# Loading K and V two units at a time: 1 MB transfers, four ring and five kept buffers, and another mix of phases

## The chip, the cores and the metric

The kernel runs on one core of one Trainium2 chip. The metric is the device time of one execution in microseconds; lower is better. Profiles are taken on the same kernel in an execution of its own. All runs used below are in the fast state.

## The reference, cut to what matters

Two layers of attention over a cached K and V, each followed by a small gated feed-forward, for four batches with one new token each. Both attention layers read the same cache.

```python
B, Sq, D = 4, 1, 512
Hq, Hkv, Sk, Dh = 32, 8, 8192, 128
x = A_x
x = x + _A_ref(_layernorm(x), A_k_cache, A_v_cache, A_wq, A_wo)
x = x + _B_ref(_layernorm(x), B_w_gate, B_w_up, B_w_down)
x = x + _A_ref(_layernorm(x), A_k_cache, A_v_cache, A_wq, A_wo)
x = x + _B_ref(_layernorm(x), B_w_gate, B_w_up, B_w_down)
```

K and V have 67 MB each in bfloat16, and each is needed twice. So nearly all the work is bringing some 260 MB in from HBM, and TensorE must keep up with it.

## The kernel before

The cache is cut into units: 2,048 positions of one head, 512 KB, so 16 blocks of 128 x 128. A key unit is transposed block by block on TensorE, copied out of PSUM by VectorE or ScalarE in two halves, and multiplied with the padded query. A value unit takes 16 matmuls of 4 columns.

```python
CR = 2048; NRING = 7; NRET = 11
ring = sb("ring", [P, NRING, NB * Dh], BF16)     # buffers of one unit, 4 KB for each partition
kept = sb("kept", [P, NRET, NB * Dh], BF16)      # value units of layer 1 that layer 2 uses again
...
def pump():                                      # issue loads in order while their buffer is free
    while lptr[0] < len(loads):
        ...
            ap, key = home[x]
            if not released.get(key, True):
                return
            src = cache[b, g, c * CR:(c + 1) * CR, :].rearrange("(p t) d -> p (t d)", p=P)
            T.dma("sp", ap, src, sm, writes=[key])
...
def k_front(u):
    ap, key = home[u]
    for hf in range(2):
        for t in range(8):
            ... matmul(stg[:, t * P:(t + 1) * P], lhsT=ap[:, blk * Dh:(blk + 1) * Dh],
                       rhs=ident[:], is_transpose=True, ...)   reads=[key, "ident"]
        evac(ktp[:, s, :], stg[:, :], ...)
    release(u)
```

The helper `T` follows who reads and writes each named buffer and puts the waits in: TensorE waits for a buffer's transfer, and the transfer that refills the buffer waits for the last matmul that read it.

The units are used in an order cut into phases. A1 has the keys of layer 1 for batch 0; B1 has values of batch 0 among keys of batch 1; then for each batch C1 (the feed-forward of layer 1 with some value units as filler), A2 (keys of layer 2 with some values) and B2 (values of layer 2 among keys of a later batch in layer 1). `NFILL` is the number of value units in C1, `TAIL1` and `TAIL2` the number left to the end of a phase, `LEAD` the number at its start, `FL` how the fillers lie between the steps of the feed-forward, and `DP`, `DL`, `DQ` delay steps of the softmax and of the query projection by so many units.

Of the kernel before, what the change touches and what calls it, by code (L numbers as in the profile page):

```python
# [7 lines left out]
BF16 = mybir.dt.bfloat16  # L8
# [94 lines left out]
def bass_interleave_layers__gqa_block_cached__swiglu_ffn__decode_kernel(  # L103
# [12 lines left out]
    B, _, D = A_x.shape  # L116
    _, G, S, Dh = A_k_cache.shape
# [4 lines left out]
    P = 128  # L122
# [4 lines left out]
    CR = 2048  # L127
    NB = CR // P
    NJ = 4
    NM = NB // NJ  # L130
    NCH = S // CR
    BW = 512
    NRING = 7
    NRET = 11
    NKT = 4
    scale = float(Dh) ** -0.5
    EPS = 1e-5
# [1 line left out]
    with ExitStack() as es:  # L139
        sb = lambda name, shape, dt: es.enter_context(nc.sbuf_tensor(name, shape, dt))  # L140
# [2 lines left out]
        wg_sb = sb("wg_sb", [P, KT, F], BF16)  # L143
        wu_sb = sb("wu_sb", [P, KT, F], BF16)
        wd_sb = sb("wd_sb", [P, FO, D], BF16)
        ring = sb("ring", [P, NRING, NB * Dh], BF16)
        kept = sb("kept", [P, NRET, NB * Dh], BF16)
        ktp = sb("ktp", [P, NKT, 8 * P], BF16)
        pp = sb("pp", [P, 3, S // NJ], BF16)
        qpad1 = sb("qpad1", [P, B, G, 32], BF16)  # L150
# [33 lines left out]
        us = sb("us", [P, FO * B], FP32)  # L184
# [17 lines left out]
        sem_ring = [sem(f"sem_ring{i}") for i in range(NRING)]  # L202
        sem_kept = [sem(f"sem_kept{i}") for i in range(NRET)]
# [3 lines left out]
        T = _Sync(engines, prog)  # L207
# [41 lines left out]


        def KU(l, b, c):
            return [("k", l, b, g, c) for g in range(G)]

        def VU(l, b, g):
            return [("v", l, b, g, c) for c in range(NCH)]

        kept_ix = {}
        for g in range(G):
            for c in range(NCH):
                if len(kept_ix) < NRET:  # L260
                    kept_ix[(g, c)] = len(kept_ix)

# [11 lines left out]

        A_of = lambda l, b, cs: sum((KU(l, b, c) for c in cs), [])
        B_of = lambda l, b, gs: sum((VU(l, b, g) for g in gs), [])
        TAIL1 = [9, 9, 6]
        TAIL2 = [4, 5, 5, 6]
        NFILL = [12, 16, 16, 12]
        LATE = [8, 8, 16]  # L280
        LEAD = [4, 4]
        ECUT = [0, 0, 0, 0]
        FL = (1, 2, 1, 1, 2, 1, 2, 2)
        V1O = [[3, 4, 5, 6, 7, 0, 1, 2]] * 4
        V2O = [[3, 0, 4, 1, 5, 2, 6, 7]] * 2 + [[3, 0, 1, 2, 4, 5, 6, 7]] + [[3, 0, 4, 1, 5, 2, 6, 7]]
        DP = 1
        DL = 2
        DO = 4
        DQ = 1

        def split(us, n):
            return us[:len(us) - n], us[len(us) - n:]
# [7 lines left out]
        for b in range(B):  # L300
# [12 lines left out]
            else:  # L313
                early = []
            phases.append(("B2", b, v2))
        order = [u for _, _, us in phases for u in us]
        assert len(set(order)) == len(order) == 4 * B * G * NCH


        group_phases = {}  # L320
# [9 lines left out]
        loads = []  # L330
        home = {}
        nring = 0
        for n, u in enumerate(order):
            kind, l, b, g, c = u
            if kind == "v" and (g, c) in kept_ix:
                s = kept_ix[(g, c)]
                home[u] = (kept[:, s, :], f"kept{s}")
                if l == 0:
                    loads.append(("unit", u, sem_kept[s]))
            else:  # L340
                s = nring % NRING
                nring += 1
                home[u] = (ring[:, s, :], f"ring{s}")
                loads.append(("unit", u, sem_ring[s]))

        wpieces = []
        for k in range(4):
# [7 lines left out]
            fs = slice(k * FO // 2, (k + 1) * FO // 2)  # L355
            wpieces.append((wd_sb[:, fs, :], B_w_down.rearrange("(fo p) n -> p fo n", p=P)[:, fs, :], f"wd{k}"))
        for k, w in enumerate(wpieces):
            at = 8 + 5 * k
            loads.insert(at, ("w", w, sem(f"sem_{w[2]}")))

        released = {}
# [2 lines left out]
        def pump():  # L364
            while lptr[0] < len(loads):
                kind, x, sm = loads[lptr[0]]
                if kind == "w":
                    T.dma("sp", x[0], x[1], sm, writes=[x[2]])
                else:
                    ap, key = home[x]  # L370
                    if not released.get(key, True):
                        return
                    released[key] = False
                    _, l, b, g, c = x
                    cache = A_k_cache if x[0] == "k" else A_v_cache
                    src = cache[b, g, c * CR:(c + 1) * CR, :].rearrange("(p t) d -> p (t d)", p=P)
                    T.dma("sp", ap, src, sm, writes=[key])
                lptr[0] += 1

        def release(u):  # L380
            key = home[u][1]
            if key.startswith("kept") and u[1] == 0:
                return
            released[key] = True


        kt_ctr = [0]
# [10 lines left out]
                    delayed.append((n - 1, f))  # L398

        def k_front(u):  # L400
            ap, key = home[u]
            halves = []
            for hf in range(2):
                bk = next_bank()
                stg = bank_bf(bk)
                for t in range(8):
                    blk = hf * 8 + t
                    T.op("pe", lambda e: e.matmul(stg[:, t * P:(t + 1) * P], lhsT=ap[:, blk * Dh:(blk + 1) * Dh],  # L408
                                                  rhs=ident[:], is_transpose=True, start=True, stop=True),
                         reads=[key, "ident"], writes=[f"pb{bk}"], sig=(t == 7))  # L410
                s = kt_ctr[0] % NKT
                kt_ctr[0] += 1
                evac(ktp[:, s, :], stg[:, :], reads=[f"pb{bk}"], writes=[f"kt{s}"])
                halves.append(s)
            release(u)
            return halves
# [82 lines left out]
        def v_unit(u):  # L499
            _, l, b, g, c = u  # L500
            q = pbuf[(l, b)]
            ap, key = home[u]
            bk = pv_bank[u[:4]]
            for m in range(NM):
                for j in range(NJ):
# [290 lines left out]
```

## Time and profile before

| | before |
|---|---|
| median, range | 700.16 us, 696.73 to 702.53 (3 runs) |
| profiled run | 701.5 us, span 699.7 us, mean clock 0.811 |
| TensorE busy | 584.9 us of the span |
| bytes moved | 260.9 MB, mean 373 GB/s |

The lines on which the reading rests stand in the prediction. Two more views are needed later. First, the transfers (out<-in, count, size, median time from issue to landing), from the page:

```profile
ring<-in_A_k_cache_dram SPq DMA_DIRECT2D x256, 512.0 KB, 7.6
ring<-in_A_v_cache_dram SPq DMA_DIRECT2D x168, 512.0 KB, 7.6
kept<-in_A_v_cache_dram SPq DMA_DIRECT2D x44, 512.0 KB, 12.2
```

A 512 KB transfer takes 7.6 us from issue to landing but one lands every 1.28 us in a busy stretch: some six are under way at a time. Second, the waits of TensorE for a landing (us in total, times, longest):

```profile
PE ps L408 <- DMA ring<-in_A_k_cache_dram: 35.0, 44, 2.7
PE ps L507 <- DMA ring<-in_A_v_cache_dram: 6.7, 11, 1.1
PE ps L507 <- DMA kept<-in_A_v_cache_dram: 6.3, 11, 0.8
```

TensorE waits 48 us for landings in all, most of it for keys. The prediction took these as waits of an engine that is not the bound.

### The profile page before, as it was taken

How to read it: one execution, taken by the hardware profiler on the slowest of the kernel's cores; microseconds unless marked ns; L12 is line 12 of the kernel's file. 1: busy time of each engine (PE TensorE's matmuls, PEld its weight loads, DVE VectorE, ACT ScalarE, POOL GpSimd, SP SyncE). 2: the span in 40 equal slices, each digit the busy share in tenths (PEclk: the TensorE clock that was granted, in tenths of full speed). 3: DMA queues.
4: the chain of work that ended last, by engine and by line, in shares of the span. 5: the costliest groups of instructions: out<-in, count | busy, mean ns of one | idle time of the engine just before them, and what ended most of it. 6: DMA issues, size and time to landing. Idle time of an engine off the chain costs nothing.

```text
span 699.7 us, 25539 instructions
## 1 busy us (share of the span) xinstructions
PE 584.9 (84%) x11552; PEld 479.2 (68%) x11552; DVE 298.8 (43%) x635; ACT 235.1 (34%) x296; POOL 0.7 (0%) x6
## 2 busy tenths in 40 slices
PE   3977879878699899987799898988799876799876
PEld 2755657657677687766677677767777675777665
DVE  1544524443156645452165534543155510266501
ACT  1533324331056434420154434432055500055400
POOL 0000000000000000000000000000000000000000
PEclk9999879995589889985599879995589955599855
DMA  8999999999889999999999999999899989999992
GB/s 349 388 388 408 385 395 407 401 401 409 328 284 411 404 399 407 406 408 392 335 343 409 402 370 385 370 409 407 320 382 409 408 325 410 349 338 361 343 396 75
DMA packets 75117, 260.93 MB, mean 373 GB/s; under 512 B 7672, under 2 KB 13568, under 8 KB 74496
## 3 DMA queue, kind: packets, MB, share of 16 engines
q1 hardware_dynamic: 75008, 259.30, 96.1%
q8 instruction: 90, 1.47, 0.9%
q14 instruction: 19, 0.16, 0.1%
HBM read 259.26 MB, written 0.00 MB: 371 GB/s over the span
## 4 chain that ended last, share of the span: by engine, by line
PE 51%; DMA 37%; issue 5%; DVE 4%; ACT 2%; SPq 1%; ACTq 0%
DMA ring<-in_A_k_cache_dram 27%; PE ps L408 25%; PE ps L507 9%; DMA ring<-in_A_v_cache_dram 8%; PE ps L424 7%; PE ps L572 3%; PE ps L596 2%; DMA wq_sb<-in_A_wq_dram 2%; PE ps L531 1%; SPq L92 1%; PE ps L632 1%; PE ps L548 1%; ACT ktp L248 1%; PE ps L479 1%; DVE negm L436 1%
## 5 line engine op out<-in xcount | busy, mean ns | idle before, releaser
L408 PE MATMUL ps<-ident,ring 128*128 128x128 bf16 x4096 | 294.6, 230 | 36.8 <-DMA ring<-in_A_k_cache_dram 35.0
L408 PEld LDWEIGHTS ps<-ident,ring 128*128 128x128 bf16 x4096 | 251.4, 103 | 79.0 <-DMA ring<-in_A_k_cache_dram 54.1
L246 DVE COPY ktp<-ps 128x1024 bf16<-128x1024 bf16 x320 | 215.6, 689 | 206.3 <-PE ps L408 205.4
L248 ACT ACTIVATE ktp<-ps 128x1024 bf16<-128x1024 bf16 x192 | 195.5, 1023 | 259.7 <-PE ps L408 259.7
L424 PE MATMUL ps<-ktp,qpad 128*32 128x512 bf16 x1024 | 111.3, 401 | 3.3 <-ACT ktp L248 2.6
L507 PE MATMUL ps<-pp,ring 128*128 128x4 bf16 x2688 | 88.9, 166 | 22.5 <-issue 13.1
L507 PEld LDWEIGHTS ps<-pp,ring 128*128 128x128 bf16 x2688 | 82.5, 102 | 35.5 <-issue 21.8
L424 PEld LDWEIGHTS ps<-ktp,qpad 128*32 128x32 bf16 x1024 | 27.7, 93 | 37.7 <-ACT ktp L248 7.5
L507 PE MATMUL ps<-pp,kept 128*128 128x4 bf16 x1408 | 45.8, 166 | 8.7 <-DMA kept<-in_A_v_cache_dram 6.3
L507 PEld LDWEIGHTS ps<-pp,kept 128*128 128x128 bf16 x1408 | 41.4, 101 | 16.6 <-DMA kept<-in_A_v_cache_dram 7.9
L564 ACT ACTIVATE lnv<-var,eps_sb 128x4 f32<-128x4 f32 x10 | 3.0, 297 | 142.9 <-DVE var L551 142.9
L515 DVE TENSOR_TENSOR oT<-ps,invL 128x4 bf16<-128x4 f32 x64 | 10.6, 166 | 79.8 <-PE ps L507 79.7
L438 ACT ACTIVATE pp<-ps,negm 128x512 bf16<-128x512 f32 x32 | 22.0, 687 | 26.7 <-DVE negm L436 22.7
L572 PE MATMUL ps<-xnT,wq_sb 128*128 128x4 bf16 x640 | 18.7, 166 | 11.5 <-DMA wq_sb<-in_A_wq_dram 7.7
L436 DVE TENSOR_REDUCE negm<-ps 128x1 f32<-128x512 f32 x32 | 22.1, 690 | 11.6 <-PE ps L424 10.0
L572 PEld LDWEIGHTS ps<-xnT,wq_sb 128*128 128x128 bf16 x640 | 17.9, 104 | 12.0 <-DMA wq_sb<-in_A_wq_dram 7.8
L531 PE MATMUL ps<-oT,wo_sb 128*128 128x4 bf16 x640 | 21.3, 166 | 5.5 <-DVE oT L515 2.9
L531 PEld LDWEIGHTS ps<-oT,wo_sb 128*128 128x128 bf16 x640 | 20.0, 104 | 7.8 <-issue 4.7
L479 PE MATMUL ps<-ident,pp 128*128 128x128 bf16 x128 | 14.5, 303 | 1.3 <-DVE pp L469 1.0
L551 DVE TENSOR_REDUCE var<-ps 128x4 f32<-128x16 f32 x10 | 1.7, 175 | 28.2 <-PE ps L548 28.2
L479 PEld LDWEIGHTS ps<-ident,pp 128*128 128x128 bf16 x128 | 12.4, 140 | 1.9 <-DVE pp L469 1.7
L248 ACT ACTIVATE pp<-ps 128x1024 bf16<-128x1024 bf16 x6 | 6.1, 1025 | 16.8 <-PE ps L479 16.8
(66 smaller groups left out, 158.1 us busy)
## 6 DMA issues: line engine op xcount, KB each, us to landing
ring<-in_A_k_cache_dram SPq DMA_DIRECT2D x256, 512.0 KB, 7.6
ring<-in_A_v_cache_dram SPq DMA_DIRECT2D x168, 512.0 KB, 7.6
kept<-in_A_v_cache_dram SPq DMA_DIRECT2D x44, 512.0 KB, 12.2
wq_sb<-in_A_wq_dram SPq DMA_DIRECT2D x1, 4096.0 KB, 12.4
wo_sb<-in_A_wo_dram SPq DMA_DIRECT2D x4, 1024.0 KB, 11.6
wg_sb<-in_B_w_gate_dram SPq DMA_DIRECT2D x2, 896.0 KB, 12.0
wu_sb<-in_B_w_up_dram SPq DMA_DIRECT2D x2, 896.0 KB, 11.9
wd_sb<-in_B_w_down_dram SPq DMA_DIRECT2D x2, 896.0 KB, 9.2
```

Source lines behind the costliest of these rows:

```text
L246: T.op("dve", lambda e: e.tensor_copy(dst, src), reads=reads, writes=writes)
L248: T.op("act", lambda e: e.activation(dst, src, ACTF.Copy), reads=reads, writes=writes)
L408: T.op("pe", lambda e: e.matmul(stg[:, t * P:(t + 1) * P], lhsT=ap[:, blk * Dh:(blk + 1) * Dh], rhs=ident[:], is_transpose=True, start=Tru ...
L424: T.op("pe", lambda e: e.matmul(ps[32 * j:32 * (j + 1), bk * BW:(bk + 1) * BW], lhsT=qp, rhs=ktp[:, s, (j % 2) * 512:(j % 2 + 1) * 512], s ...
L436: T.op("dve", lambda e: e.tensor_reduce(negm[:, q, c:c + 1], bank(bk), AX.X, ALU.max, negate=True), reads=[f"pb{bk}"], writes=[f"negm{q}_{ ...
L438: T.op("act", lambda e: e.activation(pp[:, q, c * 512:(c + 1) * 512], bank(bk), ACTF.Exp, bias=negm[:, q, c:c + 1], scale=1.0, accum_out=l ...
L479: T.op("pe", lambda e: e.matmul(stg[:, t * P:(t + 1) * P], lhsT=pp[:, q, blk * P:(blk + 1) * P], rhs=ident[:], is_transpose=True, start=Tr ...
L507: T.op("pe", lambda e: e.matmul(ps[:, bk * BW:bk * BW + REP], lhsT=ap[:, (NM * j + m) * Dh:(NM * j + m + 1) * Dh], rhs=pp[:, q, col:col + ...
L515: T.op("dve", lambda e: e.tensor_tensor(oT[:, l, g * REP:(g + 1) * REP, b], ps[:, bk * BW:bk * BW + REP], invL[:, q, g * REP:(g + 1) * REP ...
L531: T.op("pe", lambda e: e.matmul(ps[:, OPJ * BW + nq * B:OPJ * BW + (nq + 1) * B], lhsT=wo_sb[:, h, nq * P:(nq + 1) * P], rhs=oT[:, l, h, : ...
L572: T.op("pe", lambda e: e.matmul(misc[:, h * B:(h + 1) * B], lhsT=wq_sb[:, kt, h * Dh:(h + 1) * Dh], rhs=xnT[:, kt * B:(kt + 1) * B], start ...
L596: T.op("pe", lambda e: e.matmul(ps[:, bk * BW + fo * B:bk * BW + (fo + 1) * B], lhsT=w_sb[:, kt, fo * P:(fo + 1) * P], rhs=xnT[:, kt * B:( ...
```

## The change

The intent is fewer, larger transfers: two neighbouring units (two heads of K, or two chunks of V) come in one transfer of 1 MB into a buffer of twice the size. The memory for buffers stays 18 units: before 7 + 11, now (4 + 5) x 2. The order of units, the fillers and the delays are set anew. The diff is cut; the weights keep their places in the order of loads (after 8 units, then every 4).

```diff
-    NRING = 7
-    NRET = 11
+    NRING = 4
+    NRET = 5
@@
-            return [("k", l, b, g, c) for g in range(G)]
+            return [(("k", l, b, g, c), ("k", l, b, g + 1, c)) for g in range(0, G, 2)]
@@
-            return [("v", l, b, g, c) for c in range(NCH)]
+            return [(("v", l, b, g, c), ("v", l, b, g, c + 1)) for c in range(0, NCH, 2)]
@@ (numbers now count pairs)
-        TAIL1 = [9, 9, 6]
-        TAIL2 = [4, 5, 5, 6]
-        NFILL = [12, 16, 16, 12]
-        LATE = [8, 8, 16]
-        LEAD = [4, 4]
+        TAIL1 = [5, 5, 5]
+        TAIL2 = [2, 3, 3, 3]
+        NFILL = [3, 5, 7, 2]
+        LATE = [4, 4, 8]
+        LEAD = [0, 4]
-        FL = (1, 2, 1, 1, 2, 1, 2, 2)
+        FL = [0, 2, 1, 0, 2, 1, 2, 2]
-        DP = 1
-        DL = 2
+        DP = 3
+        DL = 3
-        DQ = 1
+        DQ = 0
@@
+            for i, u in enumerate(pr):
+                home[u] = (buf[:, i * NB * Dh:(i + 1) * NB * Dh], key, i == 1)
@@
+                    if kind == "k":
+                        src = A_k_cache[b, g:g + 2, c * CR:(c + 1) * CR, :].rearrange("i (p t) d -> p i (t d)", p=P)
+                    else:
+                        src = A_v_cache[b, g, c * CR:(c + 2) * CR, :].rearrange("(i p t) d -> p i (t d)", i=2, p=P)
+                    T.dma("sp", buf.rearrange("p (i x) -> p i x", i=2), src, sm, writes=[key])
@@
-            released[key] = True
+            _, key, end = home[u]
+            if end and not (key.startswith("kept") and u[1] == 0):
+                released[key] = True
```

Both units of a pair share one name (`key`). So TensorE waits for the whole transfer before the first unit, and the refill waits for the second unit.

More of the change, by code (lines that the diff above doesn't have):

```diff
@@ L145, in bass_interleave_layers__gqa_block_cached__swiglu_ffn__decode_kernel @@
         wd_sb = sb("wd_sb", [P, FO, D], BF16)
-        ring = sb("ring", [P, NRING, NB * Dh], BF16)
-        kept = sb("kept", [P, NRET, NB * Dh], BF16)
+        ring = sb("ring", [P, NRING, 2 * NB * Dh], BF16)
+        kept = sb("kept", [P, NRET, 2 * NB * Dh], BF16)
         ktp = sb("ktp", [P, NKT, 8 * P], BF16)
@@ L251, in KU @@
         def KU(l, b, c):
-            return [("k", l, b, g, c) for g in range(G)]
+            return [(("k", l, b, g, c), ("k", l, b, g + 1, c)) for g in range(0, G, 2)]
         def VU(l, b, g):
-            return [("v", l, b, g, c) for c in range(NCH)]
+            return [(("v", l, b, g, c), ("v", l, b, g, c + 1)) for c in range(0, NCH, 2)]
         kept_ix = {}
         for g in range(G):
-            for c in range(NCH):
+            for c in range(0, NCH, 2):
                 if len(kept_ix) < NRET:
@@ L276, in bass_interleave_layers__gqa_block_cached__swiglu_ffn__decode_kernel @@
         B_of = lambda l, b, gs: sum((VU(l, b, g) for g in gs), [])
-        TAIL1 = [9, 9, 6]
-        TAIL2 = [4, 5, 5, 6]
-        NFILL = [12, 16, 16, 12]
-        LATE = [8, 8, 16]
-        LEAD = [4, 4]
+        TAIL1 = [5, 5, 5]
[3 more added lines that the diff above has]
+        LEAD = [0, 4]
+        WAT = 4
+        WSTEP = 3
         ECUT = [0, 0, 0, 0]
-        FL = (1, 2, 1, 1, 2, 1, 2, 2)
+        FL = [0, 2, 1, 0, 2, 1, 2, 2]
         V1O = [[3, 4, 5, 6, 7, 0, 1, 2]] * 4
         V2O = [[3, 0, 4, 1, 5, 2, 6, 7]] * 2 + [[3, 0, 1, 2, 4, 5, 6, 7]] + [[3, 0, 4, 1, 5, 2, 6, 7]]
-        DP = 1
-        DL = 2
+        DP = 3
+        DL = 3
         DO = 4
-        DQ = 1
+        DQ = 0
         def split(us, n):
@@ L315, in bass_interleave_layers__gqa_block_cached__swiglu_ffn__decode_kernel @@
             phases.append(("B2", b, v2))
-        order = [u for _, _, us in phases for u in us]
-        assert len(set(order)) == len(order) == 4 * B * G * NCH
+        order = [pr for _, _, prs in phases for pr in prs]
+        assert len(set(order)) == len(order) == 2 * B * G * NCH
+        phases = [(name, b, [u for pr in prs for u in pr]) for name, b, prs in phases]
+        vseq = [u for _, _, us_ in phases for u in us_ if u[0] == "v"]
+        assert all(len(set(u[:4] for u in vseq[i:i + NCH])) == 1 for i in range(0, len(vseq), NCH))
         group_phases = {}
@@ L332, in bass_interleave_layers__gqa_block_cached__swiglu_ffn__decode_kernel @@
         nring = 0
-        for n, u in enumerate(order):
-            kind, l, b, g, c = u
+        for pr in order:
+            kind, l, b, g, c = pr[0]
             if kind == "v" and (g, c) in kept_ix:
                 s = kept_ix[(g, c)]
-                home[u] = (kept[:, s, :], f"kept{s}")
-                if l == 0:
-                    loads.append(("unit", u, sem_kept[s]))
+                buf, key, sm = kept[:, s, :], f"kept{s}", sem_kept[s]
+                fresh = l == 0
             else:
@@ L342, in bass_interleave_layers__gqa_block_cached__swiglu_ffn__decode_kernel @@
                 nring += 1
-                home[u] = (ring[:, s, :], f"ring{s}")
-                loads.append(("unit", u, sem_ring[s]))
+                buf, key, sm = ring[:, s, :], f"ring{s}", sem_ring[s]
+                fresh = True
+            for i, u in enumerate(pr):
+                home[u] = (buf[:, i * NB * Dh:(i + 1) * NB * Dh], key, i == 1)
+            if fresh:
+                loads.append(("unit", (pr, buf, key), sm))
         wpieces = []
@@ L357, in bass_interleave_layers__gqa_block_cached__swiglu_ffn__decode_kernel @@
         for k, w in enumerate(wpieces):
-            at = 8 + 5 * k
+            at = WAT + WSTEP * k
             loads.insert(at, ("w", w, sem(f"sem_{w[2]}")))
@@ L369, in pump @@
                 else:
-                    ap, key = home[x]
+                    pr, buf, key = x
                     if not released.get(key, True):
@@ L373, in pump @@
                     released[key] = False
-                    _, l, b, g, c = x
-                    cache = A_k_cache if x[0] == "k" else A_v_cache
-                    src = cache[b, g, c * CR:(c + 1) * CR, :].rearrange("(p t) d -> p (t d)", p=P)
-                    T.dma("sp", ap, src, sm, writes=[key])
+                    kind, l, b, g, c = pr[0]
+                    if kind == "k":
[3 more added lines that the diff above has]
+                    T.dma("sp", buf.rearrange("p (i x) -> p i x", i=2), src, sm, writes=[key])
                 lptr[0] += 1
         def release(u):
-            key = home[u][1]
-            if key.startswith("kept") and u[1] == 0:
-                return
-            released[key] = True
+            _, key, end = home[u]
+            if end and not (key.startswith("kept") and u[1] == 0):
+                released[key] = True
         kt_ctr = [0]
@@ L400, in k_front @@
         def k_front(u):
-            ap, key = home[u]
+            ap, key, _ = home[u]
             halves = []
@@ L501, in v_unit @@
             q = pbuf[(l, b)]
-            ap, key = home[u]
+            ap, key, _ = home[u]
             bk = pv_bank[u[:4]]
```

## The prediction

> **What bounds the kernel now.** I read the page's slices first, then the queue table, then the chain, then a table of stretches cut at the kernel's own phases (found from the order of the transpose and value matmuls on TensorE), then the timeline of one stretch.
>
> ```profile
> DMA  8999999999889999999999999999899989999992
> GB/s 349 388 388 408 385 395 407 401 401 409 328 284 411 404 399 407 406 408 392 335 343 409 402 370 385 370 409 407 320 382 409 408 325 410 349 338 361 343 396 75
> DMA packets 75117, 260.93 MB, mean 373 GB/s; under 512 B 7672, under 2 KB 13568, under 8 KB 74496
> q1 hardware_dynamic: 75008, 259.30, 96.1%
> ```
>
> The queue's packets are being served for 96.1% of the span, and the best slices stop at 408 to 411 GB/s. So this is a kernel on a DMA ceiling with dips. 259.3 MB at 408 GB/s would take 636 us.
>
> The packet records of the trace, taken by size, give the ceiling more exactly. There are 59,904 packets of 4 KB, median 159 ns, and 7,672 of 4 bytes, 9 ns each: the completion marks, 16 per transfer. The weights are 5,896 of 1 KB (48 ns), 1,024 of 3.5 KB (144 ns) and 512 of 8 KB (309 ns). 90 instruction blocks of 16 KB take 1,069 ns. Times counts over 16 engines: 595.3 + 4.3 + 17.7 + 9.2 + 9.9 + 6.0 = 643 us with the few rest. The span is 700, so 57 us are lost to the ceiling. Where, the phase table shows (columns: stretch, its length, busy time and count of PE, PEld, DVE, ACT, POOL; clock, DMA share, GB/s):
>
> ```profile
> 81.20:167.80 86.60, 72.32 (x1303) 58.13 (x1304) 34.92 (x65) 29.01 (x35) 0.00 (x0) 0.84 1.02 398
> 167.80:190.30 22.50, 16.92 (x549) 16.45 (x547) 4.53 (x24) 1.25 (x5) 0.00 (x0) 0.50 0.95 356
> 190.30:246.20 55.90, 52.66 (x828) 40.98 (x826) 32.97 (x57) 29.01 (x34) 0.00 (x0) 0.90 0.95 365
> 246.20:318.90 72.70, 65.56 (x1287) 52.99 (x1288) 35.23 (x67) 27.44 (x33) 0.00 (x0) 0.90 1.02 405
> ...
> 609.70:663.30 53.60, 50.11 (x731) 37.51 (x728) 33.47 (x58) 27.33 (x33) 0.00 (x0) 0.95 0.94 343
> 663.30:699.70 36.40, 25.29 (x818) 23.95 (x817) 4.71 (x23) 0.75 (x3) 0.00 (x0) 0.50 0.63 238
> ```
>
> These are B1, C1 (feed-forward of layer 1), A2 (keys of layer 2), B2, and at the end A2 and B2 of the last batch. For each phase I subtract its packets at the times above from its length. A1 loses 2.4 us, B1 1.2, the first three B2 6.6 together, the four pairs C1+A2 8.8, 7.7, 5.4 and 9.9 (31.8), and the last phase 15.0, of which 12.2 follow the last landing. So A1, B1 and B2 run at the DMA ceiling. C1 and A2 don't: there TensorE sets the pace (52.66 of 55.90 us busy) and the queue waits for full buffers. In C1 it is also short of instructions:
>
> ```profile
> 173.17 1.37 PE L596 MATMUL ps<-xnT,wu_sb 128*128 128x4 bf16 x46
> 176.86 0.43 PE L596 MATMUL ps<-xnT,wu_sb 128*128 128x4 bf16 x10 [2.33 <-issue]
> ...
> 212.64 1.07 PE L408 MATMUL ps<-ident,ring 128*128 128x128 bf16 x16
> 213.63 0.40 PE L424 MATMUL ps<-ktp,qpad 128*32 128x512 bf16 x4
> 213.97 1.07 PE L408 MATMUL ps<-ident,ring 128*128 128x128 bf16 x16
> 214.96 0.40 PE L424 MATMUL ps<-ktp,qpad 128*32 128x512 bf16 x4
> 215.29 0.55 PE L507 MATMUL ps<-pp,ring 128*128 128x4 bf16 x16
> 215.71 1.05 PE L408 MATMUL ps<-ident,ring 128*128 128x128 bf16 x16
> ```
>
> The first two lines show a group of 56 cut by 2.33 us in which nothing but issue is waited for. Such gaps sum to 19.4 us over the four C1. From start to start, a key unit costs TensorE 1.33 us (212.64 to 213.97) and a value unit 0.42 (215.29 to 215.71). A 512 KB transfer costs the queue 8 x 159 + 9 = 1,281 ns per engine. Keys alone are slower on TensorE than on DMA by 0.05 us; a value unit gives the queue 0.86 us of work ahead.
>
> **What the Trainium skill says.** "DMA: Bandwidth & Descriptors", Rules for kernel authors, asks for at least 1 MiB per DMA, and its Measured table has 341 GB/s for 1 MB against 425 for 16 MB, with some 2 us of fixed cost per DMA. That is a transfer alone. The trace disagrees for queued ones: 512 KB transfers sustain 407 GB/s from 270 to 300 us, since six are in flight (7.6 us to landing over 1.28 each). The fixed part that does not overlap here is the 9 ns mark; the rest is the 159 ns packet, whose size stays. "HBM Reference", Bandwidth, gives about 425 GB/s for a core alone, bounded by its DMA engines: the 8 KB packets of wq reach 423 (5 to 13 us), the 4 KB ones do not. "Runtime: NRT & Kernel Launch", Instruction fetch mechanics, says that instructions come in blocks of 16 KiB (256 instructions), mostly hidden. The 90 packets of 16 KB agree; that they hide does not hold in C1. "TensorE: Matmul & The Clock Gate", Part 1, has half clock after an idle window of some 3.4 us; the trace has 0.50 in all of C1, with a value unit at the same 0.42 there.
>
> **The change part by part.**
> 1. *Transfers.* 468 units of 512 KB (256 + 168 + 44) become 236 of 1 MB. The key source keeps runs of 4 KB (two heads), and the value source too (two chunks, each split over partitions). So the same packets, and 232 marks per engine fewer: 232 x 9 ns = -2.1 us.
> 2. *Kept buffers.* 11 units become 10, so one value unit per batch is loaded twice: 4 x 1.27 = +5.1 us. Floor: 643 - 2.1 + 5.1 = 646.
> 3. *Ring.* 7 units become 8, but a buffer returns only after its second unit. Ahead of a busy TensorE there are still six whole units, seven or more in the first half of a pair. Where DMA binds, TensorE starts a pair when both have landed: at each end of such a phase one more unit stands after the landing (0.42 us for values, 1.33 for keys at the end of A1). I put +1 us on the six DMA-bound stretches in all.
> 4. *Mix.* The units used in C1 fall from 12, 16, 16, 12 to 6, 10, 14, 4, and those of A2 rise from 40, 44, 44, 36 to 46, 50, 46, 44; the sum of each pair stays. So 22 value units move. C1 loses 22 x 0.42 = 9.3 us of TensorE work and A2 gains the same. C1 also loses 22 x 32 = 704 instructions, 2.75 blocks, at some 1.8 us a stall: about -5. With fewer fillers, waits for VectorE show in C1: 1 us in each of two, about 0.5 in the others, +3. In A2 the blocks are hidden, and the queue gains 22 x 1.28 us of work just where it was idle, though TensorE sets the time there. Net about -2 for the pairs, and another -2 at the end: the last A2 leaves less to load, where the queue was idle for 8.6 us and then set the pace up to the landing at 687.5.
> 5. *Delays* (DP 3, DL 3, DQ 0): these move the softmax chain behind more value units; I put 0. The weights keep their places (after 8 units, then every 4).
> 6. *Tail.* One value unit more after the last landing: +0.4.
>
> Sum: 700.2 - 2.1 + 5.1 + 1 - 2 - 2 + 0.4 = 700.6. The mix and delays were evidently tuned for the new size, and 31.8 us lost in C1 and A2 leave room for more than I can derive; for that I take off 3.6 by judgement: 697.
>
> **Rivals.** *Bigger transfers run faster.* If packets became 8 KB as in wq, 59,904 x 159 would turn into half as many of 309 ns: -17 us, 680, faster by nearly 3%. For it: 423 against 407 GB/s. Against: neither side's source has 8 KB runs. *Coarse release starves or cools TensorE.* With KKKKVV in lumps, a value pair leaves 1.7 us of waiting, clock windows may fall to 0.50, where a key unit takes 2.4 us against 1.28 of DMA; four phases with a few such lumps are +8 to +12, 709. For it: clock 0.84 already in B1. Against: a cold pair lump (KKVV, 5.7 us) is only 0.5 longer than its DMA (5.1) and rewarms. *The mix frees A2 wholly.* If value units in A2 let both engines run full, half of 31.8 is won: 684. Against: TensorE's work in C1+A2 is the same, and it is what binds there.
>
> **Range and chances.** The derived sum and the judgement give 697. The second rival bounds the high side near 709, the third the low side near 684; 2% is 686 and 714. Faster by over 2% needs the first or third rival nearly whole: 0.13. Slower needs more than the second: 0.05.
>
> **What would show it.** Right: 236 transfers of 1 MB, some 7 to 10 us from issue to landing; 4 KB packets still 159 ns; steady stretches at 408 to 412 GB/s; some 261.4 MB; issue gaps in C1 shorter by a few us; A2 longer but with a higher GB/s than 343 to 392. Wrong: 8 KB packets or over 418 GB/s in steady stretches; B phases below 390 GB/s or a clock under 0.8 in them; C1 as long as before with waits for VectorE in it.

## The result, and the profile after

Ratios here and below are the mean time of one kernel's fast runs over that of the other's in the same rounds on the same chip, so they are not quite the ratio of the medians quoted beside them.

| | before | changed |
|---|---|---|
| median, range | 700.62 us, 696.73 to 702.53 (4 runs) | 722.51 us, 719.64 to 727.74 (4 runs) |
| ratio, 95% interval | | 1.0328, 1.0249 to 1.0408: slower |
| profiled span, clock | 699.7 us, 0.811 | 718.7 us, 0.799 |

The time went up by over 3%, above the range of the prediction (near 684 to near 709). First the page of the changed kernel, the lines that answer to those of the prediction:

```profile
DMA  8999999999699999999899999999999989599992
GB/s 350 388 388 407 397 399 375 403 401 386 235 374 398 363 353 399 352 411 393 294 391 399 384 403 382 385 409 402 314 386 383 393 339 408 181 370 389 370 402 80
DMA packets 71914, 262.99 MB, mean 366 GB/s; under 512 B 3960, under 2 KB 9856, under 8 KB 71296
q1 hardware_dynamic: 71808, 261.38, 94.9%
```

The best slices are no faster than before (411 GB/s in both), so larger transfers gave the queue no speed. What is new is the slices between 352 and 399 where before stood 401 to 411, and two deep ones of 235 and 181. The queue is served for a smaller share of a longer span.

The parts of the floor (all packet times, divided by the 16 engines) came out as worked out. The packet records have 60,416 packets of 4 KB (512 more, the four extra value units), again of median 159 ns, and 3,960 of 4 bytes (3,712 fewer, which is 232 x 16), again of 9 ns. The floor is 646 us. So 718.7 - 646 = 73 us are lost to it, where it was 57.

The table of stretches at the changed kernel's own phases (stretch, length, busy and count of PE, PEld, DVE, ACT, POOL; clock, DMA share, GB/s): B1, C1, A2 and B2 of the first batch, then the last A2 and B2.

```profile
82.40:170.20 87.80, 73.85 (x1304) 58.99 (x1304) 35.03 (x66) 28.85 (x35) 0.00 (x0) 0.81 1.02 395
170.20:183.70 13.50, 11.00 (x352) 10.75 (x353) 3.38 (x18) 0.79 (x4) 0.00 (x0) 0.50 0.98 367
183.70:251.50 67.80, 61.02 (x1019) 48.05 (x1017) 33.97 (x62) 29.48 (x36) 0.00 (x0) 0.85 0.91 341
251.50:329.80 78.30, 69.74 (x1290) 56.74 (x1291) 35.70 (x68) 27.66 (x33) 0.00 (x0) 0.83 1.00 381
...
615.80:679.60 63.80, 58.11 (x918) 44.63 (x919) 34.59 (x64) 27.83 (x35) 0.00 (x0) 0.87 0.88 327
679.60:718.70 39.10, 25.71 (x816) 23.99 (x816) 4.36 (x22) 0.75 (x3) 0.00 (x0) 0.50 0.65 250
```

C1 is shorter, as the mix intended: 13.5 us in this batch, not 22.5. But A2 grew from 55.9 to 67.8, and its rate fell from 365 to 341 GB/s where a rise was forecast. The third line from the top has it all: more value units to load, a lower rate, a lower clock. And B2, which ran at 405 GB/s, now runs at 381; a B phase below 390 was a sign of being wrong in the prediction. One of its signs of being right came true too: the gaps of "issue" in the four C1 sum to 9.8 us, not 19.4.

TensorE's waits for landings (us in total, times, longest) are these:

```profile
PE ps L417 <- DMA ring<-in_A_k_cache_dram: 42.0, 38, 2.8
PE ps L516 <- DMA ring<-in_A_v_cache_dram: 13.5, 13, 1.6
PE ps L516 <- DMA kept<-in_A_v_cache_dram: 6.2, 7, 1.6
```

62 us, 14 more than before, in fewer but longer waits. Last, a stretch of TensorE's timeline in B2 (start, length, line, what; in brackets the idle time before it and what ended it):

```profile
276.32 0.95 PE L516 MATMUL ps<-pp,ring 128*128 128x4 bf16 x32
278.64 1.07 PE L417 MATMUL ps<-ident,ring 128*128 128x128 bf16 x16 [1.37 <-DMA ring<-in_A_k_cache_dram]
279.63 0.40 PE L433 MATMUL ps<-ktp,qpad 128*32 128x512 bf16 x4
279.97 1.72 PE L417 MATMUL ps<-ident,ring 128*128 128x128 bf16 x16
281.61 0.62 PE L433 MATMUL ps<-ktp,qpad 128*32 128x512 bf16 x4
282.16 1.01 PE L516 MATMUL ps<-pp,ring 128*128 128x4 bf16 x32
283.74 1.89 PE L417 MATMUL ps<-ident,ring 128*128 128x128 bf16 x16 [0.56 <-DMA ring<-in_A_k_cache_dram]
```

TensorE finishes a value pair at 277.3 and stands idle until 278.6, when a key pair lands whole. Then two key units stand before it at once. The clock falls in the middle of them: the transposes of the second unit take 1.72 us, not 1.07.

Two suspects remain. *Lumps*: landing or returning two units at a time. *Mix*: the new order, fillers and delays. The clock could be a part of either.

### The profile page after: what moved, and what is told of

The parts are those of the page before. It is cut to its first block, busy times and chain, and to the rows that moved or that the text cites. A ratio compares the mean times of both kernels' runs of the same rounds, so it can differ in the third digit from the quotient of the medians.

```text
span 718.7 us, 25091 instructions
## 1 busy us (share of the span) xinstructions
PE 595.8 (83%) x11552; PEld 486.6 (68%) x11552; DVE 299.5 (42%) x635; ACT 235.4 (33%) x296; POOL 0.7 (0%) x6
## 2 busy tenths in 40 slices
DMA packets 71914, 262.99 MB, mean 366 GB/s; under 512 B 3960, under 2 KB 9856, under 8 KB 71296
## 3 DMA queue, kind: packets, MB, share of 16 engines
q1 hardware_dynamic: 71808, 261.38, 94.9%
## 4 chain that ended last, share of the span: by engine, by line
PE 46%; DMA 45%; DVE 3%; issue 3%; SPq 1%; ACT 1%; ACTq 0%
DMA ring<-in_A_k_cache_dram 29%; PE ps L417 24%; DMA ring<-in_A_v_cache_dram 14%; PE ps L516 6%; PE ps L433 6%; PE ps L581 2%; DMA wq_sb<-in_A_wq_dram 2%; PE ps L605 2%; SPq L92 1%; PE ps L557 1%; PE ps L641 1%; PE ps L540 1%; PE ps L488 1%; DVE negm L445 1%; ACT ktp L248 1%
## 5 line engine op out<-in xcount | busy, mean ns | idle before, releaser
L417 PE MATMUL ps<-ident,ring 128*128 128x128 bf16 x4096 | 303.4, 233 | 42.3 <-DMA ring<-in_A_k_cache_dram 42.0
L417 PEld LDWEIGHTS ps<-ident,ring 128*128 128x128 bf16 x4096 | 258.9, 105 | 94.7 <-DMA ring<-in_A_k_cache_dram 52.7
L433 PE MATMUL ps<-ktp,qpad 128*32 128x512 bf16 x1024 | 113.8, 414 | 3.5 <-ACT ktp L248 3.0
L516 PE MATMUL ps<-pp,ring 128*128 128x4 bf16 x2816 | 88.6, 166 | 27.1 <-DMA ring<-in_A_v_cache_dram 13.5
L516 PE MATMUL ps<-pp,kept 128*128 128x4 bf16 x1280 | 39.5, 166 | 8.9 <-DMA kept<-in_A_v_cache_dram 6.2
L516 PEld LDWEIGHTS ps<-pp,kept 128*128 128x128 bf16 x1280 | 37.6, 103 | 11.7 <-issue 6.1
L581 PE MATMUL ps<-xnT,wq_sb 128*128 128x4 bf16 x640 | 18.7, 166 | 10.9 <-DMA wq_sb<-in_A_wq_dram 7.8
L540 PEld LDWEIGHTS ps<-oT,wo_sb 128*128 128x128 bf16 x640 | 19.4, 102 | 7.1 <-issue 3.6
L641 PE MATMUL ps<-hT,wd_sb 128*128 128x4 bf16 x280 | 8.5, 166 | 5.0 <-issue 3.8
## 6 DMA issues: line engine op xcount, KB each, us to landing
wg_sb<-in_B_w_gate_dram SPq DMA_DIRECT2D x2, 896.0 KB, 13.5
```

The source lines that it names most:

```text
L417: T.op("pe", lambda e: e.matmul(stg[:, t * P:(t + 1) * P], lhsT=ap[:, blk * Dh:(blk + 1) * Dh], rhs=ident[:], is_transpose=True, start=Tru ...
L433: T.op("pe", lambda e: e.matmul(ps[32 * j:32 * (j + 1), bk * BW:(bk + 1) * BW], lhsT=qp, rhs=ktp[:, s, (j % 2) * 512:(j % 2 + 1) * 512], s ...
L516: T.op("pe", lambda e: e.matmul(ps[:, bk * BW:bk * BW + REP], lhsT=ap[:, (NM * j + m) * Dh:(NM * j + m + 1) * Dh], rhs=pp[:, q, col:col + ...
L540: T.op("pe", lambda e: e.matmul(ps[:, OPJ * BW + nq * B:OPJ * BW + (nq + 1) * B], lhsT=wo_sb[:, h, nq * P:(nq + 1) * P], rhs=oT[:, l, h, : ...
L581: T.op("pe", lambda e: e.matmul(misc[:, h * B:(h + 1) * B], lhsT=wq_sb[:, kt, h * Dh:(h + 1) * Dh], rhs=xnT[:, kt * B:(kt + 1) * B], start ...
L641: T.op("pe", lambda e: e.matmul(misc[:, nq * B:(nq + 1) * B], lhsT=wd_sb[:, fo, nq * P:(nq + 1) * P], rhs=hT[:, fo * B:(fo + 1) * B], star ...
```

## The experiments

Each run was timed in three rounds against the kernel before, 4 to 20 executions each. The slow executions of the kernel before are left out: one of 1080 us in the rounds of e13 to e15, and four of 704 to 705 us in the others. All of the experiments' own executions are fast. All results agreed with the reference within its tolerance, also those of e13 to e15, which leave out a part of the work.

| run | what differs | median us | ratio to before (95%) |
|---|---|---|---|
| changed | | 722.5 | 1.0328 (1.0249 to 1.0408) |
| e1 | new mix; transfers and buffers of before | 712.5 | 1.0208 (1.0153 to 1.0263) |
| e2 | changed, 512 KB units, 8 ring and 10 kept | 706.1 | 1.0118 (1.0051 to 1.0186) |
| e3 | changed, mix of before | 722.5 | 1.0359 (1.0298 to 1.0419) |
| e4 | changed, each transfer cut in two | 704.3 | 1.0086 (1.0064 to 1.0107) |
| e5 | only key transfers cut | 707.4 | 1.0114 (1.0066 to 1.0162) |
| e6 | only value transfers cut | 716.1 | 1.0252 (1.0163 to 1.0341) |
| e7 | changed, extra matmuls to hold the clock | 722.1 | 1.0327 (1.0263 to 1.0390) |
| e8 | e4 with the mix of before | 699.1 | 1.0014 (0.9993 to 1.0035) |
| e9 | e4, halves refilled together | 707.8 | 1.0177 (1.0143 to 1.0210) |
| e10 | e4, TensorE waits for both halves | 721.2 | 1.0358 (1.0288 to 1.0429) |
| e11 | e8, value pairs whole with 8 KB runs | 702.6 | 1.0098 (1.0061 to 1.0134) |
| e12 | changed, 8 KB runs for keys and values | 716.6 | 1.0299 (1.0261 to 1.0336) |
| e13 | changed, half the transposes | 702.4 | 1.0035 (1.0015 to 1.0055) |
| e14 | e4, half the transposes | 690.1 | 0.9846 (0.9814 to 0.9878) |
| e15 | e12, half the transposes | 692.0 | 0.9888 (0.9852 to 0.9924) |

### First: lumps or mix (e1 to e4)

**e1: the new mix alone.** The transfers, ring 7 and kept 11 of before, and the order, fillers and delays of the change.

```diff
 # on the changed kernel
-    NRING = 4; NRET = 5         # buffers of two units
+    NRING = 7; NRET = 11        # buffers of one unit
-        for pr in order:
+        for u in [u for pr in order for u in pr]:
+            home[u] = (buf, key, True)          # one transfer, one buffer, one semaphore for each unit
```

> The new order of units and the new delays, but transfers of 512 KB, a ring of 7 and 11 kept buffers as before. If the 1 MB lumps cause the loss (theory 'lumps'): 694 to 703 us, ratio to before 0.99 to 1.005. If the new mix or delays cause it (theory 'mix'): 714 to 724 us, ratio 1.02 to 1.035. Half and half would be near 710.

It came out at 1.0208, between the two. So the mix is not harmless with the buffers of before.

**e2: only the transfer size undone.** As e1, but with 8 ring and 10 kept units, which are the bytes and the memory of the change.

> The changed kernel with only the transfer size undone: same order, same bytes (10 kept units, so 5 us more on the DMA floor than before), ring of 8 units of 512 KB, each landing and returned alone. Theory lumps: 699 to 707 us. Theory mix: 718 to 726 us. The difference from e1 is the price of the four more units loaded (5.1 us by my sum) less what the eighth buffer gives.

1.0118: 2.1% below the change, with the same order and the same bytes. That is the lumps. And it is below e1 although it loads 5 us more (the intervals just overlap). My guess is that the new mix, which uses fewer units in C1, needs the eighth ring buffer; no run tests it.

**e3: the lumps with the mix of before.**

```diff
-        TAIL1 = [5, 5, 5]; NFILL = [3, 5, 7, 2]; LEAD = [0, 4]
-        FL = [0, 2, 1, 0, 2, 1, 2, 2]; DP = 3; DL = 3; DQ = 0
+        TAIL1 = [5, 5, 3]; NFILL = [6, 8, 8, 6]; LEAD = [2, 2]
+        FL = [1, 2, 1, 1, 2, 1, 2, 2]; DP = 1; DL = 2; DQ = 1
```

> 1 MB transfers with ring 4 and 5 kept, but the mix, fillers and delays of before (numbers of units rounded to pairs). Theory lumps: 716 to 730 us, as slow as the change or slower, since the mix had been tuned for it. Theory mix: 700 to 708 us (5 us of bytes, -2 of marks).

1.0359, as slow as the change. The mix is not what makes the change slow, and it doesn't rescue it either: the intervals overlap. ("The mix of before" here and in e8 is rounded to pairs: keys and values still come in twos.)

**e4: each 1 MB transfer in two.** Two transfers of 512 KB into the halves of a pair buffer, each with a semaphore of its own. The order is unchanged.

```diff
-                    T.dma("sp", buf.rearrange("p (i x) -> p i x", i=2), src, sm, writes=[key])
+                    for i, (kind, l, b, g, c) in enumerate(pr):
+                        src = cache[b, g, c * CR:(c + 1) * CR, :].rearrange("(p t) d -> p (t d)", p=P)
+                        T.dma("sp", buf[:, i * NB * Dh:(i + 1) * NB * Dh], src, sm[i], writes=[f"{key}_{i}"])
```

> The changed kernel with each 1 MB transfer cut in two of 512 KB into the same pair buffer, each with its own semaphore; the buffer still returns only after its second unit. If late landing is what costs (TensorE waits for two units where one would do): 704 to 710 us. If late return is what costs (the queue has fewer transfers in flight behind a full ring): 716 to 723 us, as the change. If the mix does it all: as the change.

1.0086: 2.4% below the change, some 17 us. The text on record says that the buffer "still returns only after its second unit". That was wrong. The halves have names of their own, so the refill of the first half waits only for the first unit; the trace shows the two halves refilled at different times. So e4 lands and returns early, and e9 and e10 had to part the two.

TensorE's waits in e4 (us in total, times, longest):

```profile
PE ps L416 <- DMA ring<-in_A_k_cache_dram: 25.4, 28, 2.8
PE ps L515 <- DMA ring<-in_A_v_cache_dram: 13.5, 24, 0.8
PE ps L515 <- DMA kept<-in_A_v_cache_dram: 6.9, 8, 1.6
```

The waits for keys are 25.4 us, against 42.0 in the changed kernel. Those for values are nearly the same. These 16.6 us are near the difference of the two spans (718.7 and 702.0), but the match is luck: TensorE's idle time of every kind differs by 11.5 us, and its busy time, for the same matmuls, by 5.2 (595.8 and 590.6).

### Which transfers, and the clock (e5 to e8)

**e5: only the key transfers cut; e6: only the value transfers cut.**

> The changed kernel with only the key transfers cut in two of 512 KB (own semaphores, same pair buffers); values still land 1 MB at a time. Theory 'keys' (a late key pair leaves TensorE 2.66 us of work to do behind the landing, a value pair only 0.84): 703 to 709 us, most of the 18 us that both cuts together won. Theory 'both alike': 710 to 716. Theory 'values': 717 to 723.

> The mirror: only the value transfers cut in two, key pairs land whole. Theory keys: 716 to 722 us. Both alike: 710 to 716. Theory values: 703 to 709. If the two do not add up to the 18 us of the full cut, they act on the same wait.

Keys cut alone give 1.0114, values cut alone 1.0252. Of the 2.4% between the change and e4, the keys give 2.1 and the values 0.8, a bit more than the whole together. So it is mostly the keys; the gain of the values alone is not clear of noise, since e6's interval overlaps that of the change. A likely reason, argued and not tested: behind a late key pair stand 2.66 us of TensorE work, behind a value pair 0.84.

**e7: hold the clock up.** Three matmuls of 448 columns into unused PSUM columns after each value pair before a key, in B1 and B2.

```diff
+                T.op("pe", lambda e: e.matmul(ps[:, OPJ * BW + 64:OPJ * BW + 512], lhsT=ident[:],
+                                              rhs=wq_sb[:, 0, 0:448], start=True, stop=True, ...))
```

> The changed kernel with three extra matmuls of 448 columns into unused columns of a bank after each value pair that is followed by a key, in B1 and B2 only (31 places, 0.56 us each at full clock, 17 us of TensorE work that should lie in waits for DMA). If the clock falling to one half during the lumpy waits causes most of the loss (theory 'clock'): 706 to 714 us and the short half-clock stretches (17 of them, 82 us, against 11 and 51 in the cut-in-two kernel) go below 10. If the wait itself is the loss (theory 'wait'): 719 to 728 us, whatever the clock does; what the clock can give by the key units' transposes alone (245.4 us in all against 240.9) is 4 to 5 us.

The clock did as asked. The clock records have 9 stretches of less than 20 us at one half, with 55 us in all, where the changed kernel has 17 with 82 us. From the start of a unit's first transpose to that of its last, 28 key units took over 1.2 us, not 39, and all keys together 237.1 us, not 245.4. The time did not move: 1.0327. The extra matmuls (17 us by their starts, only in B1 and B2) may have cost something of their own where no wait lay, so several us of clock are not excluded by this run alone. As the main cause of the 3% nothing speaks for it, and e10 below speaks against it.

**e8: e4 with the mix of before.**

> Pair buffers, transfers cut in two, with the mix and delays of before. It differs from before by four more units loaded (+5 us), an eighth ring unit, late return and the rounding to pairs. If the new mix is worth something once landing is early: 705 to 712 us, above the 704 of the new mix. If the new mix is worth nothing or costs: 698 to 704.

1.0014: the time of before, with four more units loaded. Against e4 (1.0086) the new mix costs 0.7%, some 5 us, where units land alone. And against e3, which differs from e8 by the whole transfers only, the lumps cost 3.4%, some 23 us.

### Landing or return (e9, e10)

**e9: halves land alone, but are refilled together.**

```diff
+                    T.wait_res("sp", writes=[f"{key}_0", f"{key}_1"])
                     for i, (kind, l, b, g, c) in enumerate(pr):
```

**e10: halves are refilled alone, but TensorE waits for both before the first unit** (in the key and in the value routine).

```diff
+            T.wait_res("pe", reads=[key[:-2] + "_0", key[:-2] + "_1"])
```

> e4 needs a second look: its two halves of a buffer were tracked apart, so a half was not only waited for alone, it was also refilled as soon as its own unit was done. Here the halves land alone, but the refill of both waits until the second unit is done, as with 1 MB transfers. If landing is what counts: 703 to 707 us, as e4 (704.3). If the return is: 715 to 722. In between, each has its share, to be read off together with e10.

> The mirror: each half is refilled as soon as its own unit is done, but TensorE waits for both halves before the first unit. If landing counts: 716 to 723 us, as the change. If the return counts: 703 to 708. If the loss only comes when both are late (each alone is bridged by the other): both e9 and e10 stay below 712.

Late return alone: 1.0177, 0.9% above e4. Late landing alone: 1.0358, no better than the change. So the landing is the main cause, and the return a smaller one that no longer shows once the landing is late (1.0328 with both, 1.0358 with one; the intervals overlap). The e10 runs are spread (714.7 to 724.3) and its profiled run was the shortest of them, so its trace shows less than the usual loss. One thing can be read from it all the same. It is 10.9 us longer than e4's (712.9 and 702.0) at the same mean clock (0.806 and 0.805), with TensorE busy for 587.9 us, not 590.6. So late landing costs time without any fall of the clock; this idles TensorE for 13.6 us more.

### Longer runs in the packets (e11, e12)

**e11 was meant to gain.** On e8, value pairs in one transfer with one run of 8 KB for each partition; keys in 512 KB, taken at a pitch of 8 KB so that both use the same order of positions. **e12** gives the changed kernel runs of 8 KB for keys (two chunks of one head) and values.

```diff
-  A_v_cache[b, g, c * CR:(c + 2) * CR, :].rearrange("(i p t) d -> p i (t d)", i=2, p=P)
+  A_v_cache[b, g, c * CR:(c + 2) * CR, :].rearrange("(p x) d -> p (x d)", p=P)
-  A_k_cache[b, g:g + 2, c * CR:(c + 1) * CR, :].rearrange("i (p t) d -> p i (t d)", p=P)     # e12 only
+  A_k_cache[b, g, c * CR:(c + 2) * CR, :].rearrange("(p x) d -> p (x d)", p=P)
```

> A version meant to gain: old mix, keys in 512 KB transfers, value pairs in 1 MB with one run of 8 KB for each partition (keys taken at a pitch of 8 KB so that both use the same order of positions). Against e8 (699.1): 13,824 packets of 8 KB at 309 ns in place of 27,648 at 159 take 7.8 us from the floor; late value landings give back about 3 (e5 less e4). Expected 692 to 697 us. If the floor does not set the time, 699 to 703.

> The changed kernel, whole 1 MB transfers and new mix, but both keys (two chunks of one head) and values with runs of 8 KB for each partition. 30,208 packets of 309 ns in place of 60,416 of 159: 17 us off the floor. If the floor and the late landing add up: 703 to 709 us. If late landing eats what a faster queue gives: 714 to 722. If the packets don't reach 309 ns, that shows in the packet records.

Neither gained. e11 is 1.0098, 0.8% above e8. e12 is 1.0299, only 0.3% below the change (6 us by the medians, but the kernel before was faster in e12's rounds too; the intervals overlap). Both fell into the range that their text gives for the case against a gain. The packets did what they should: the page of e12 shows them, and its packet records have 8 KB at a median of 309 ns.

```profile
DMA packets 41706, 262.99 MB, mean 367 GB/s; under 512 B 3960, under 2 KB 9856, under 8 KB 10880
q1 hardware_dynamic: 41600, 261.38, 92.9%
```

The queue is busy for 92.9%, where the changed kernel has 94.9%. Most of the 17 us off the floor turned into idle time of the queue. So with pairs that land whole the floor by packets does not set the time; the premise of my prediction does not hold in the form I gave it. One thing is not parted: e12's keys also come in another order (two chunks of one head), and by phases of the profiled execution it is 8.0 us shorter than the changed kernel in C1 and A2 and 5.0 longer in the first three B2. e11 keeps the order of keys but lets value pairs land whole.

### Giving TensorE slack (e13 to e15)

Why does late landing reach the end of the span? Either TensorE has hardly any slack behind a landing (balance), or the queue itself suffers from lumps whatever TensorE does. In these kernels only 8 of the 16 blocks of a key unit are transposed, and half-size copies made. The result is wrong on purpose (it passes the comparison all the same, presumably since the scores are small and the softmax is nearly flat). Not shown: the unused half of each copy's buffer is set to zero once.

```diff
-                for t in range(8):
+                for t in range(4):
-                evac(ktp[:, s, :], stg[:, :], reads=[f"pb{bk}"], writes=[f"kt{s}"])
+                evac(ktp[:, s, 0:512], stg[:, 0:512], reads=[f"pb{bk}"], writes=[f"kt{s}"])
```

> A wrong result on purpose: the changed kernel with only half of each key unit's blocks transposed and copied (8 transposes and half-size copies per unit; some 0.5 us less of TensorE per key unit, 128 us in all). Theory balance: TensorE has slack, the queue keeps full, and landing late costs little: within 5 us of e14, both 655 to 680 us. Theory queue: 12 us or more above e14.

> A wrong result on purpose: e4 (halves land alone) with the same cut in TensorE's work. 655 to 680 us in both theories; the floor is 648 and the end of some 12 us behind the last landing stays.

> A wrong result on purpose: e12 (runs of 8 KB, whole 1 MB transfers) with the same cut. Theory balance: with slack on TensorE the packets' 17 us show, so 12 to 17 us below e13. If it is no more than 4 below e13, the floor by packet times is not what holds the time, even with TensorE relieved.

None fell to 680 us. The relief was smaller than planned: TensorE's busy time in e13 is 522 us, not some 470, and the mean clock fell from 0.80 to 0.70. e13 is 1.9% above e14 (12 us), where the pair with full work is 2.4% apart. And e15 is 1.5% below e13, some 10 us of the 17, where e12 was 0.3% below the change. TensorE's waits for keys in e13 and then in e14 (us in total, times, longest):

```profile
PE ps L418 <- DMA ring<-in_A_k_cache_dram: 86.4, 70, 3.7
```

```profile
PE ps L417 <- DMA ring<-in_A_k_cache_dram: 58.1, 83, 3.3
```

(With the values' waits it is 119 us and 104.) So both hold in part. With slack on TensorE faster packets begin to pay: balance. But even then landing and returning whole costs 12 us, the mark that was set for the other theory, so it is not only a matter of TensorE's own load.

## Why the prediction was wrong

**The step that failed is number 3, the ring.** It said: "Where DMA binds, TensorE starts a pair when both have landed: at each end of such a phase one more unit stands after the landing", and put "+1 us on the six DMA-bound stretches in all". Measured, landing and returning in whole pairs is worth 17 to 23 us (the change against e4, e3 against e8). Late landing alone is worth as much as both (e10 against e4, 17 us by the medians), late return alone 3 to 6 (e9 against e4, by medians and by ratios). The kind of cost was named, one unit that stands after a landing, but it was charged once for each phase. The trace charges it each time TensorE catches up with the landings. The step's other half, the amount of loads ahead, was right: from 100 to 150 us, in B1, 3.3 transfers of 1 MB are under way on average, against 6.5 of 512 KB before.

I compared the start of the same units in the changed kernel and in e4. The lag doesn't grow evenly. In the first A2 it is at most 1.1 us up to 203 us. Then TensorE waits for two key pairs, at 205.8 and 211.1 us, and it goes up by 0.97 and 0.92 us. In the changed kernel (start, length, line, what; idle time before):

```profile
205.81 1.07 PE L417 MATMUL ps<-ident,ring 128*128 128x128 bf16 x16 [0.83 <-DMA ring<-in_A_k_cache_dram]
...
211.08 1.15 PE L417 MATMUL ps<-ident,ring 128*128 128x128 bf16 x16 [1.66 <-DMA ring<-in_A_k_cache_dram]
212.15 0.62 PE L433 MATMUL ps<-ktp,qpad 128*32 128x512 bf16 x4
212.70 1.89 PE L417 MATMUL ps<-ident,ring 128*128 128x128 bf16 x16
```

and the same two units in e4:

```profile
203.70 1.05 PE L416 MATMUL ps<-ident,ring 128*128 128x128 bf16 x16
...
208.04 1.07 PE L416 MATMUL ps<-ident,ring 128*128 128x128 bf16 x16 [0.70 <-DMA ring<-in_A_k_cache_dram]
```

The next rise, 1.34 us up to 215.1, is no wait: it is a stretch at half clock (1.89 us for the transposes at 212.7, not 1.07) that follows the longer wait. e4 has none there. The same comes again at 231.8 us: 0.43 from a wait, then 1.49 from half clock. About 1.4 us is won back in between, where DMA has run ahead, and A2 ends with a lag of 4.8. So in this stretch the clock enlarges what the landing starts; e10 shows that it is not needed for a loss.

By phases (from the matmul starts; one profiled execution each):

| phases | before | changed | e4 | e8 |
|---|---|---|---|---|
| A1 and B1 | 167.8 | 170.2 | 167.5 | 166.7 |
| the four pairs C1 + A2 | 322.9 | 326.2 | 316.1 | 319.8 |
| the first three B2 | 172.6 | 183.1 | 178.6 | 174.2 |
| the last B2 | 36.4 | 39.1 | 39.8 | 38.3 |

Against the kernel before, 10.5 of the 19 us lie in the first three B2. Of the 16.7 us between the changed kernel and e4, which differ in the transfers alone, 10.1 lie in C1 + A2 and 4.5 in B2. How it comes about shows in the same stretches of both traces, at the head, the middle and the end of the first A2 (columns as above). First the changed kernel, then e4:

```profile
180.00:185.00 5.00, 4.52 (x104) 4.42 (x102) 1.46 (x8) 0.50 (x2) 0.00 (x0) 0.50 0.95 356
185.00:190.00 5.00, 5.00 (x96) 4.37 (x94) 2.04 (x4) 1.02 (x1) 0.00 (x0) 0.50 0.05 17
...
200.00:205.00 5.00, 4.98 (x84) 3.56 (x80) 3.71 (x6) 3.63 (x5) 0.00 (x0) 1.00 0.96 304
...
240.00:245.00 5.00, 3.24 (x52) 2.13 (x50) 2.27 (x5) 2.54 (x4) 0.00 (x0) 1.00 0.94 347
```

```profile
180.00:185.00 5.00, 4.69 (x115) 4.63 (x113) 1.31 (x5) 0.77 (x3) 0.00 (x0) 0.50 0.48 188
185.00:190.00 5.00, 5.00 (x87) 4.37 (x85) 1.96 (x4) 0.76 (x1) 0.00 (x0) 0.51 0.52 143
...
200.00:205.00 5.00, 5.00 (x87) 3.69 (x84) 3.32 (x6) 3.13 (x6) 0.00 (x0) 1.00 1.02 415
...
240.00:245.00 5.00, 3.65 (x84) 3.55 (x85) 2.10 (x8) 0.30 (x1) 0.00 (x0) 0.61 1.02 405
```

At the head the ring is full in both, while TensorE is slow (half clock). The changed kernel's dip is deeper from 185 to 190 us (17 GB/s, against 143), but e4's comes earlier: from 180 to 200 us the changed kernel moves more, 247 GB/s against 227. So the head is not where it loses. From 200 to 245 us it moves less, 384 against 409. From the issues and landings of the trace, around 200 us the changed kernel has one or two transfers on the way when it issues another, e4 four to six of half the size. That alone doesn't set the slow kernel apart: the kernel before and e8 have two or three of 512 KB there, and 356 and 300 GB/s from 200 to 205. At 205.8 TensorE waits for a pair, while e4 has begun its first half without a wait. That wait delays the return of the buffer, and so the next issue, and at 240 us the rate is still 347. In e4 (and, by their transfers, in the kernel before and in e8) TensorE works on one unit while the next one lands. In the changed kernel it waits for two and then has two to do, and the queue has to wait for free buffers. That the wait and the refill feed each other is my reading of the trace; the runs show only that both landing and return cost, and that landing costs more.

**"So A1, B1 and B2 run at the DMA ceiling" was too simple.** It let me treat 48 us of waits for landings as free. e12 took 17 us from the floor and gained 2 by the ratios. Work taken from TensorE paid more, though not in full: half the transposes gave 20 us in the changed kernel (e13, TensorE busy for 74 us less) and 14 in e4 (e14, 64 less). TensorE is busy for 84% and DMA for 96%, and each waits for the other in turn through a buffer of some 7 or 8 units.

**Steps 1 and 2, transfers and kept buffers, were right**: the packets, their times, the marks and the extra bytes came out as worked out. The ceiling did not rise, so the first rival was rightly turned down; even where its packets were made to happen (e12), the gain was 2 us, not 17. One reference is put right: the 425 GB/s of "HBM Reference" stand under Specifications (TRN2), not under a section Bandwidth.

**Step 4, the mix, was right for C1 + A2 and wrong for the rest.** It had -2 for the pairs, -2 at the end and 3.6 more by judgement. With early landing the new mix (with its delays) costs 5 us by the ratios (e4 against e8). By the phases above it gains 3.7 us in C1 + A2 and loses 4.4 in the first three B2, which the step left out, and 1.5 in the last, where it had a gain; these are differences of single executions. With whole transfers it is worth at most a few us (e3 against the change, intervals overlap): C1 did shrink, from 22.5 to 13.5 us in the first batch, but A2 took the time back with 11.9 us more. "The mix and delays were evidently tuned for the new size" was a guess, and no run bears it out.

**Step 5, the delays**, was not tried alone. **Step 6, the tail**, is inside what the last B2 shows: 39.1 us, 39.8 in e4; nothing can be read from that about 0.4 us.

**The second rival came nearest**: "Coarse release starves or cools TensorE", at 709. It was mis-sized and its stress was wrong. It rested on the clock, for which e7 found no gain, and on the release, which is the smaller part. The starving is real and was worth more than the 8 to 12 us it was given.

**Still open**: why whole pairs cost 12 us even with half the transposes (e13 against e14), how many us the falls of the clock add, and why the new mix loses in B2. No version beat the kernel before; e8 equals it.

## What to carry to other kernels

When transfers are already queued several deep, making them larger gains only the fixed cost for each one (here 9 ns in 1,281), while the consumer waits for the larger piece each time it catches up. Keep large buffers if you like, but let each part land on a semaphore of its own and go back on its own: the change against e4 and e3 against e8 show 17 to 23 us of 700 in that alone. And an engine that waits often in a "DMA-bound" stretch is not free: where two engines alternate through a small ring, shorten each in turn (here the packets in e12, the transposes in e13 and e14) before you charge the other's waits at zero.

## What the Trainium skill lacked or had wrong

- "DMA: Bandwidth & Descriptors", Rules for kernel authors, asks for at least 1 MiB per DMA. With six transfers of 512 KB under way the queue does 407 GB/s, and 1 MB transfers gave no more (best slice 411 before and after). The page doesn't set against it the cost of landing and returning in larger pieces: 3.4% here (e3 against e8). "Perfetto Trace Analysis", DMA Optimizations, does say that splitting may let some work start sooner, but ties the gain to DMA engines that are generally idle; here the queue was served for 94.9% of the span, and splitting still gained 2.4% (e4). The Measured table doesn't part transfer size from run length; here the run decided the packet: 4 KB in 159 ns, 8 KB in 309, so 412 and 424 GB/s over 16 engines.
- "Runtime: NRT & Kernel Launch", Instruction fetch mechanics, calls the refill mostly hidden. In the C1 phases, with matmuls of 4 columns, gaps of up to 2.6 us with nothing but issue to wait for sum to 19.4 us of the span before. In the packet records of the first two C1, a block of 16 KB is on its way at the start of four of the five longest gaps and starts within half a microsecond at the fifth, so the refill is the likely cause.
- "TensorE: Matmul & The Clock Gate", Part 1, speaks of idle and busy windows, but not of how much work makes a window busy. Here the clock is 0.50 all through C1 with TensorE busy for 16.92 of 22.50 us, and with half the transposes the mean clock went from 0.80 to 0.70.
